# A fused windowed attention and SwiGLU kernel on one Trainium2 core: the first keys by the hardware DMA queues in fp32, and a new order of the second group's turns

## The chip, the cores and the metric

The kernel runs on one core of a Trainium2 chip. The metric is the device time of one execution in microseconds (us). Timed runs come in rounds with the kernel before, and each ratio has a 95% interval. Profile times are us from the start of the profiled execution's span. The span is about 1.7 us shorter than the time of the run.

## The reference

```python
# q, k, v: (4, 8, 768, 64) float32; n_sink = 4, window = 128
scores = scale * q @ k^T
keep   = (key position < n_sink) or (0 <= query position - key position < window)
a      = softmax(where(keep, scores, -1e9))
x      = (a @ v), heads side by side: 3072 tokens x 512
g      = x @ w_gate; val = x @ w_val          # 512 -> 1536
out    = (silu(g) * val) @ w_out              # 1536 -> 512, float32
```

## The kernel before

Tokens are handled in 12 groups of 256. Keys and queries arrive with tokens on the partitions and are "turned" by TensorE: a small matmul with an identity matrix transposes each block, then ScalarE (keys) or VectorE (queries) copies it from PSUM to SBUF as bf16. One "pair" is two heads. Group 0 opens the kernel, so its turns cannot begin before its first keys and queries have landed. The parts that matter here:

```python
# loads of group 0
nat[0] = natp.tile([P, H, 4 * D], BF16, tag="kq", name="kq")
for k2 in range(2):                       # keys: two cast loads, fp32 to bf16
    hs = slice(4 * k2, 4 * k2 + 4)
    nc.gpsimd.dma_start(nat[0][0:64, hs], four_tokens(k, 0, hs))
first = []
for p in range(NP2):                      # queries: four plain loads, fp32
    st = opool.tile([P, 2, 4 * D], FP32, tag="ot", name="st")
    (nc.scalar, nc.sync)[p % 2].dma_start(
        st[64:P], four_tokens(q, 0, slice(2 * p, 2 * p + 2)))
    first.append(st)
# ... index patterns on GpSimd, then the values, group 1's keys and queries, weights (all cast)

# the opening, in program order (each engine keeps this order)
warm(8)                                   # matmuls of zeros
build_masks()                             # also the two identities
first_T(0)                                # turn of pair 0: keys and queries
first_T(1)
step_S(0, 0)                              # scores and exponentials, pair 0
step_S(0, 1)
first_T(2); first_T(3)                    # cut: masks between
step_S(0, 2); step_S(0, 3)
# ... probabilities times values, first half
for ph in range(2):
    step_T(1, ph, (0,))                   # group 1's keys, both halves
step_X(0, 0)                              # transpose of group 0's output
step_T(1, 0, (1,), nc.scalar.copy)        # group 1's queries, first half
step_X(0, 1)
step_T(1, 1, (1,), q_late=True)           # queries, second half
step_S(1, 0, 1)                           # scores and exponentials of group 1
```

In `step_T` the keys' copy goes to ScalarE at once. With `q_late` the queries' copy goes to VectorE after the work already put off there.

The softmax here doesn't subtract the row's maximum and nothing guards it: scores larger than these inputs give would overflow.

## Time and profile before

| what | value |
|---|---|
| time, median of 3 | 240.22 us (240.15 to 240.7) |
| profiled run | 239.81 us, span 238.1 us |
| TensorE busy | 231.4 us, 97% of the span |
| first turn starts | 4.95 us |
| first exponential starts | 6.62 us |
| group 1's first exponential starts | 14.68 us |
| dense matmuls start, on the chain | 22.97 us |

The prediction below shows the chain of waits. Two lines of the timeline of before complete it. Columns are start, length, engine, line, operation, output and input, count, and in brackets the idle time before and what ended it.

```profile
5.74 0.84 ACT L264 CAST kT<-pt 128x256 bf16<-128x256 f32 x2 [2.02 <-PE pt L258]
...
6.62 1.64 ACT L337 ACTIVATE e<-s 128x384 bf16<-128x384 f32 x4
```

ScalarE copies the keys of pairs 0 and 1 in one stretch (two copies, 0.84 us) and then begins the exponentials at once.

### The profile page before, as it was taken

How to read it: one execution, taken by the hardware profiler on the slowest of the kernel's cores; microseconds unless marked ns; L12 is line 12 of the kernel's file. 1: busy time of each engine (PE TensorE's matmuls, PEld its weight loads, DVE VectorE, ACT ScalarE, POOL GpSimd, SP SyncE). 2: the span in 40 equal slices, each digit the busy share in tenths (PEclk: the TensorE clock that was granted, in tenths of full speed). 3: DMA queues.
4: the chain of work that ended last, by engine and by line, in shares of the span. 5: the costliest groups of instructions: out<-in, count | busy, mean ns of one | idle time of the engine just before them, and what ended most of it. 6: DMA issues, size and time to landing. Idle time of an engine off the chain costs nothing.

```text
span 238.1 us, 5212 instructions
## 1 busy us (share of the span) xinstructions
PE 231.4 (97%) x2071; PEld 135.2 (57%) x2083; DVE 158.7 (67%) x337; ACT 113.3 (48%) x230; POOL 70.4 (30%) x90
## 2 busy tenths in 40 slices
PE   7899999999999999999999999999999999999994
PEld 3578887678655455544445554445454455488444
DVE  4779788749953798960798961598961599877000
ACT  2988339257732665412755622656622663333222
POOL 8976397406908049300808000000000000000000
PEclk9999999999999999999999999999999999999999
DMA  7999999997999999959999926600204200200132
GB/s 140 171 186 195 204 190 204 166 220 67 145 168 188 185 167 135 134 56 239 119 150 78 160 53 173 117 0 4 44 9 126 88 0 3 44 0 3 48 130 88
DMA packets 98936, 27.37 MB, mean 115 GB/s; under 512 B 84832, under 2 KB 95968, under 8 KB 98912
## 3 DMA queue, kind: packets, MB, share of 16 engines
q0 software_dynamic: 68832, 13.90, 70.7%
q1 hardware_dynamic: 29504, 12.69, 25.2%
q10 hardware_dynamic: 576, 0.46, 0.6%
q8 instruction: 16, 0.26, 0.4%
q14 instruction: 8, 0.07, 0.1%
HBM read 28.34 MB, written 6.29 MB: 145 GB/s over the span
## 4 chain that ended last, share of the span: by engine, by line
PE 91%; ACT 4%; DMA 2%; DVE 1%; issue 1%; DVEq 0%; POOLq 0%
PE pv L450 26%; PE pg L450 25%; PE pd L504 25%; PE o L386 5%; PE s L331 5%; ACT e L337 3%; PE pt L258 2%; DMA kq<-in_k_dram 2%; PE pd L485 1%; PE px L422 1%; DVE e L342 1%; ACT xn L394 1%; PE pk L360 1%; ACT th L457 0%; DVE qT L264 0%
## 5 line engine op out<-in xcount | busy, mean ns | idle before, releaser
L450 PE MATMUL pv<-xT,wv 128*128 128x256 bf16 (+1 forms) x384 | 74.4, 326 | 0.0
L450 PE MATMUL pg<-xT,wg 128*128 128x256 bf16 (+1 forms) x384 | 74.2, 326 | 0.0
L457 ACT ACTIVATE th<-pg 128x512 f32<-128x512 f32 x72 | 43.7, 607 | 59.7 <-PE pg L450 59.2
L464 DVE SCALAR_TENSOR_TENSOR u<-th,pg 128x512 bf16<-128x512 f32 x72 | 49.2, 683 | 30.7 <-ACT th L457 30.0
L504 PE MATMUL pd<-wo,ht 128*128 128x512 bf16 x265 | 62.4, 379 | 0.5
L465 DVE TENSOR_TENSOR ht<-u,pv 128x512 bf16<-128x512 bf16 x72 | 49.5, 688 | 9.6 <-PE pv L450 3.2
L450 PEld LDWEIGHTS <-wg 128*128 128x128 bf16 x384 | 37.4, 98 | 25.4 <-issue 0.2
L337 ACT ACTIVATE e<-s 128x512 bf16<-128x512 f32 (+1 forms) x96 | 46.2, 578 | 0.9 <-PE s L331 0.8
L450 PEld LDWEIGHTS <-wv 128*128 128x128 bf16 x384 | 34.1, 98 | 20.3 <-issue 3.6
L504 PEld LDWEIGHTS <-ht 128*128 128x128 bf16 x276 | 25.8, 98 | 28.0 <-issue 0.2
L508 ACT ACTIVATE ot<-pd 128x512 f32<-128x512 f32 x23 | 13.7, 597 | 53.2 <-PE pd L504 50.8
L342 DVE TENSOR_TENSOR e<-e,mask 128x1024 bf16<-128x1024 bf16 (+2 forms) x49 | 29.1, 631 | 2.1 <-ACT e L337 2.0
L106 POOL DMA_DIRECT2D kq<-in_k_dram x16 | 14.4, 901 | 49.2 <-DMA kqT<-kq 48.2
L122 POOL DMA_DIRECT2D va<-in_v_dram x24 | 21.6, 919 | 2.0 <-DMA kq<-in_q_dram 0.6
L398 DVE TENSOR_TENSOR xn<-o,rcp 128x256 bf16<-128x256 f32 x44 | 18.7, 425 | 4.2 <-DMA xT<-xn 2.7
L386 PEld LDWEIGHTS <-e 128*128 128x128 bf16 x352 | 16.6, 98 | 6.7 <-DVE e L342 0.9
L386 PE MATMUL o<-va,e 128*128 128x65 bf16 x352 | 18.2, 193 | 0.5 <-DVE e L342 0.4
L106 POOL DMA_DIRECT2D kq<-in_q_dram x16 | 14.5, 906 | 1.0 <-DMA wo<-in_moe_w_out_dram 1.0
L391 DVE RECIPROCAL rcp<-o 128x4 f32<-128x4 f32 x48 | 8.3, 176 | 5.3 <-PE o L386 5.1
L489 DVE TENSOR_SCALAR ot<-pd 128x128 f32<-128x128 f32 x1 | 0.3, 292 | 14.4 <-PE pd L485 14.4
L331 PE MATMUL s<-kqT 64*128 64x128 bf16 (+1 forms) x168 | 9.3, 238 | 0.0
L386 PE MATMUL o<-vsb,es 128*128 128x260 bf16 x32 | 8.8, 274 | 0.1
(59 smaller groups left out, 104.1 us busy)
## 6 DMA issues: line engine op xcount, KB each, us to landing
out_dram<-ot SPq DMA_DIRECT2D x23, 256.0 KB
va<-in_v_dram POOLq DMA_DIRECT2D x24, 128.0 KB, 6.4
kq<-in_k_dram POOLq DMA_DIRECT2D x18, 128.0 KB, 4.4
kq<-in_q_dram POOLq DMA_DIRECT2D x16, 128.0 KB, 5.2
wo<-in_moe_w_out_dram POOLq DMA_DIRECT2D x4, 384.0 KB, 12.4
wg<-in_moe_w_gate_dram POOLq DMA_DIRECT2D x4, 256.0 KB, 8.2
wv<-in_moe_w_val_dram POOLq DMA_DIRECT2D x4, 256.0 KB, 8.8
kq<-in_k_dram POOLq DMA_DIRECT2D x3, 256.0 KB, 8.9
```

What stands on the lines that cost most here:

```text
L106: nc.gpsimd.dma_start(x[:, j, i].rearrange("p (h d) -> p h d", d=D), src[b, :, t0:t0 + P].rearrange("h m d -> m h d"))
L122: nc.gpsimd.dma_start(va[:, j, :, 0:D], v[b, :, t0:t0 + P].rearrange("h m d -> m h d"))
L331: nc.tensor.matmul(pss[2 * i + h][:, col:col + n * P], keys(b, t, r, p), queries(g, r, p, j, n), start=True, stop=True)
L337: nc.scalar.activation(e_t[g][:, 2 * p + h, lo:512], pss[2 * i + h][:, lo:512], AF.Exp, scale=scale)
L342: nc.vector.tensor_tensor(e, e, m[:, :, lo:512].broadcast_to([P, e.shape[1], 512 - lo]), op=ALU.mult)
L386: nc.tensor.matmul(o, l, r, start=(i == 0), stop=(i == len(mms) - 1), skip_group_check=True)
L398: nc.vector.tensor_tensor(xns[g, j][:, 256 * hh:256 * (hh + 1)].rearrange("p (h d) -> p h d", h=4), po[:, :, 0:D], rcp.broadcast_to([P, 4, ...
L450: nc.tensor.matmul(ps[:, i * n:(i + 1) * n], ws[fi][:, c, fo * P:(fo + 1) * P], x[:, 0:n // P, c], start=(c == 0), stop=(c == DMC - 1))
L457: nc.scalar.activation(th, pg, AF.Tanh, scale=0.5)
L464: nc.vector.scalar_tensor_tensor(u, th, 1.0, pg, op0=ALU.add, op1=ALU.mult)
L465: nc.vector.tensor_tensor(hts[tb][:, f:f + two].rearrange("p a n -> p (a n)"), u, pv, op=ALU.mult)
L504: nc.tensor.matmul(po, hts[tb][:, f, ts * P:(ts + 1) * P], wos[f // n][:, f % n], start=(f == 0), stop=(f == DFC - 1))
```

## The change

The intent: keys 0 and 1 come over ScalarE's and SyncE's hardware queues instead of waiting for the software queue's cast load. Later, the second half of group 1's keys is turned together with its queries, since keys and queries use different halves of the array; this puts the first output transpose ahead of it.

```diff
-    for k2 in range(2):
-        hs = slice(4 * k2, 4 * k2 + 4)
-        nc.gpsimd.dma_start(nat[0][0:64, hs], four_tokens(k, 0, hs))
-    first = []
-    for p in range(NP2):
-        st = opool.tile([P, 2, 4 * D], FP32, tag="ot", name="st")
-        (nc.scalar, nc.sync)[p % 2].dma_start(
-            st[64:P], four_tokens(q, 0, slice(2 * p, 2 * p + 2)))
-        first.append(st)
+    nc.gpsimd.dma_start(nat[0][0:64, 4:8], four_tokens(k, 0, slice(4, 8)))
+    first = [opool.tile([P, 2, 4 * D], FP32, tag="ot", name="st") for _ in range(NP2)]
+    for n, (p, src) in enumerate(((0, q), (0, k), (1, k), (1, q), (2, q), (3, q))):
+        o = slice(0, 64) if src is k else slice(64, P)
+        (nc.scalar, nc.sync)[n % 2].dma_start(
+            first[p][o], four_tokens(src, 0, slice(2 * p, 2 * p + 2)))
     ... first_T(p): for p < 2 the keys come from first[p], with the fp32 identity
-    for ph in range(2):
-        step_T(1, ph, (0,))
+    step_T(1, 0, (0,))
     step_X(0, 0)
     step_T(1, 0, (1,), nc.scalar.copy)
     step_X(0, 1)
-    step_T(1, 1, (1,), q_late=True)
+    step_T(1, 1, q_late=True)
```

More of the change, by code (lines that the diff above doesn't have):

```diff
@@ L583, in first_T @@
     def first_T(p):
+        cast = p > 1
         evict = turn(0, (p,), (0, 1),
-                     lambda i, p: first[p] if i else nat[0][:, 2 * p:2 * p + 2],
-                     (ident, id32))
+                     lambda i, p: nat[0][:, 2 * p:2 * p + 2] if cast and i == 0 else first[p],
+                     (ident if cast else id32, id32))
         evict(0, nc.scalar.copy)
```

## The prediction

> **What bounds the kernel now.** I read first the page's busy times, to see whether one engine fills the span; then the chain of work that ended last, over the first 45 us, because the change touches only the opening; then the DMA queues in half-microsecond windows around 4 us. From the page:
>
> ```profile
> PE 231.4 (97%) x2071; PEld 135.2 (57%) x2083; DVE 158.7 (67%) x337; ACT 113.3 (48%) x230; POOL 70.4 (30%) x90
> ```
>
> TensorE is full. From the stretches of the trace, it is busy 36.95 us of the 37.00 between 23 and 60 us and 59.8 of 60 in each of the next two. So whatever the opening gains or loses moves all that follows by as much and reaches the end in full; nothing later has slack to swallow it. The opening itself is a chain over several engines:
>
> ```profile
> 1.31 3.59 DMA kq<-in_k_dram
> ...
> 4.95 0.81 PE pt L258 x21
> ...
> 5.78 0.44 DVE qT L264
> ...
> 6.26 0.37 PE s L331 x4
> 6.63 1.63 ACT e L337 x4
> 8.26 0.27 ACT kT L264
> ...
> 11.07 0.45 PE o L386 x9
> 11.52 1.01 PE pt L258 x32
> 12.53 0.33 PE px L422 x4
> 12.86 0.56 PE pt L258 x16
> 13.42 0.33 PE px L422 x4
> 13.75 0.56 PE pt L258 x16
> 14.32 0.37 PE s L331 x6
> 14.69 2.05 ACT e L337 x4
> ...
> 20.93 1.76 ACT xn L394 x8
> ...
> 22.97 0.87 PE pv L450 x8
> ```
>
> Columns are start, length and work. The cast load of group 0's first keys lands at 4.90 us; until then TensorE has no real work. After 6.63 us ScalarE's exponentials carry the chain; from 11.52 to 14.32 TensorE does (transposes of group 1's keys and queries, L258, and of group 0's output, L422); then ScalarE, VectorE and ScalarE again until 22.7 us, from where TensorE is dense. Two spots can therefore move the time: when the first exponential starts (6.63), and when group 1's first exponential starts (14.69).
>
> **What the skill says, and whether the trace agrees.** The Trainium skill, "DMA: Bandwidth & Descriptors", section "SWDGE vs HWDGE vs iDMA", gives casting during a DMA to GpSimd's software path alone. That is why the moved keys arrive in fp32. Its section "Queues, rings and completion order" says that each DMA engine goes round-robin over the queues it has work for and drains a whole packet before it switches. The trace agrees in pattern. At 3.5 to 4.0 us the software queue alone works, and at 4.0 to 4.5 us ScalarE's hardware queue (q10) gets its turn, though its second load had been issued by 2.2 us:
>
> ```profile
> q0 software_dynamic: 160, 0.08, 121.0%
> q1 hardware_dynamic: 7, 0.00, 2.6%
> ...
> q10 hardware_dynamic: 107, 0.10, 61.9%
> q0 software_dynamic: 81, 0.03, 53.1%
> q1 hardware_dynamic: 17, 0.02, 10.5%
> ```
>
> (Packets, MB, share; the first two lines are the earlier window.) The third place is "TensorE: Matmul & The Clock Gate", section "The mechanism" of part 3: matmuls on different row groups of the array overlap. The trace agrees: in group 2's turn 32 transposes, keys in one half and queries in the other, take 0.57 us (33.47 us on the chain), as long as the 16 of one kind alone at 12.86 us (0.56 us).
>
> **Part by part.**
>
> A. The loads. Before, two software cast loads bring four key pairs' halves and each hardware queue brings two fp32 query pairs. From the records of the loads' completion counts, the first key load lands at 4.90 us and the second at 6.94; the queries of ScalarE's queue land at 3.66 and 5.89, those of SyncE's at 4.29 and 6.23. Note the second loads: each lands about 2 us behind the first of its queue. After, ScalarE's queue carries queries 0, keys 1, queries 2; SyncE's carries keys 0, queries 1, queries 3; one software load brings keys 4 to 7 in the same place and at the same time (1.31 us) as the first did.
>
> A1, the first turn. It needs queries 0 (3.66), keys 0 (SyncE's first, 4.29) and the fp32 identity. The identity ends at 4.02 us now (3.37 + 0.65); it comes earlier by the 0.7 us of GpSimd's removed issue. So the first turn starts at about 4.3 instead of 4.95: 0.65 us sooner. Its 8 pairs are spaced about 0.058 us (from the starts at 5.19 to 5.77), set by the fp32 query half; an fp32 key half beside it on other rows should not lengthen that.
>
> A2, the second turn. Today it follows the first at once, since its queries come by SyncE's first load (4.29) and its keys by the load that the first turn waits for too (4.90). After the change keys 1 and queries 1 are the second loads of their queues, and I expect them where the second loads land today, 5.89 and 6.23 us. TensorE and ScalarE are in order: the second turn stands before the first scores, and both key copies on ScalarE stand before the first exponential. From the start of a turn to its copy takes 0.79 us (4.95 to 5.74), a copy 0.42 (0.84 for two). So the first exponential starts at 6.25 + 0.79 + 0.42 + 0.04 = 7.50 instead of 6.62: a loss of 0.88 us. The gain of A1 lies wholly beside this.
>
> A3, turns three and four. Queries 2 and 3 become third loads; one more round puts them near 7 to 8 us. They are needed only when the four exponentials end (7.50 + 1.64 = 9.14 us). Hidden, I think.
>
> B. Group 1's keys. Before, TensorE runs keys(both halves) 1.01, output 0.33, queries 0.56, output 0.33, queries 0.56 between 11.52 and 14.32. After, the second half's keys ride with its queries, 32 transposes in 0.57, so one stretch of about 0.5 us goes: the scores start near 13.8. But ScalarE now copies those late keys (0.56 us, 1.12 for two) just before the exponential. The turn ends near 13.85, the copy runs 13.9 to 14.47, and the exponential starts at about 14.48 instead of 14.68. B is worth 0.2 us, not 0.5; the rest becomes waiting of TensorE before 22.7 us, where ScalarE sets the pace.
>
> Sum: +0.88 - 0.20 = +0.68 us; 240.22 + 0.68 = 240.9. I take 240.8, shading toward rival 1.
>
> **Rivals.**
> 1. The second hardware loads come sooner. With keys 1 and queries 1 landed by about 5.0, the exponentials would start at 6.25 or so and the change would gain 0.4 + 0.2 = 0.6 us: 239.6. For it: removing one software load takes a competitor away, and the round-robin is inferred. Against: the surviving software load is the same size at the same time, and the second loads wait behind exactly that one.
> 2. Later still. Behind the second hardware loads now come values in 128-byte pieces rather than keys in 512-byte ones, up to 64 pieces an engine; the records show about 1075 such packets a us, so nearly 1 us for a load. If the completion of queries 1 or the third loads wait behind it, another 0.3 us goes: 241.2.
> 3. fp32 keys and fp32 queries don't overlap. Each turn would take about 0.93 instead of 0.46 us (16 x 0.058): 0.4 us more on the second turn, 241.3. The bf16 pairs' overlap speaks against it.
> 4. The transfers are hidden anyway. If ScalarE had slack before its exponentials, A would be worth nothing and B 0.2: 240.0. The chain's unbroken line from 4.95 to 6.63 us speaks against it.
>
> **Range and chances.** The terms are all under 1 us of 240, and runs of the kernel before spread from 240.15 to 240.7. Rival 1 (239.6) sets the low end; rivals 2 and 3 (241.2, 241.3) with 0.3 us of spread between runs the high one: 239.7 to 241.6. A change of 2% is 4.8 us, about as much as the whole opening waits; I give 0.005 to faster and 0.01 to slower, the rest to within 2%. Within that, slower than before has about 0.7.
>
> **What would show it.** In the profile after: the first turn starts near 4.3 us; TensorE then waits about 1.3 us on a hardware load of keys or queries between first and second turn; the first exponential starts near 7.5 us; group 1's first exponential follows ScalarE's copy of the late keys with almost no gap, near 15.2 us; the dense gate and value products start near 23.6 instead of 22.97. If the second turn starts before 5.5 us, step A2 is wrong and the time falls. If group 1's exponential starts over 0.4 us sooner after the output products than before, B is under-sized. If the span moves by more than the shift of those products, something after 23 us was touched that I held fixed, most likely the order in which weights and keys land.

## The result, and the profile after

In the first measurement the changed kernel took 240.55 us (median of 4, 240.43 to 240.76) beside 240.36 us of the kernel before. The ratio is 1.0008, interval 0.999 to 1.0025. In a second one with five rounds it took 240.95 us beside 240.29, ratio 1.0029 (1.0017 to 1.0041). A ratio is the mean time of one kernel's fast runs over the mean of the other's fast runs of the same rounds, so it is not quite the ratio of the medians quoted. Both measurements lie within 2% and within the stated range. The second is clear of 1 and puts the loss near 0.7 us.

On the page TensorE is busy 232.3 us of a span of 239.1 us, again 97%. The timeline of after shows the opening:

```profile
4.50 0.69 PE L256 MATMUL pt<-id,st 64*64 64x64 f32 x32
...
6.29 1.10 PE L256 MATMUL pt<-id,st 64*64 64x64 f32 x32 [1.09 <-DMA st<-in_k_dram]
...
7.42 0.37 ACT L262 CAST kT<-pt 128x256 bf16<-128x256 f32 x1 [1.80 <-PE pt L256]
...
7.69 1.65 ACT L335 ACTIVATE e<-s 128x384 bf16<-128x384 f32 x4
```

The first turn starts 0.45 us sooner than before. The second then waits 1.09 us for keys 1. Its copy ends the wait of ScalarE, and the first exponential starts at 7.69 instead of 6.62 us, 1.07 us later. The chain of waits of after tells the second spot (start, length, what):

```profile
4.98 8.56 DMA kq<-in_q_dram
...
13.59 0.64 PE pt L256 x16
14.22 0.33 PE px L420 x4
14.55 0.73 PE pt L256 x32
15.28 0.57 ACT kT L262
15.85 1.97 ACT e L335 x4
...
22.01 1.75 ACT xn L392 x8
...
24.04 0.87 PE pv L448 x8
```

The late keys are indeed turned together with the queries (x32). ScalarE's copy of them then stands before the exponential, as forecast. A new line leads the chain: the load of group 1's queries, issued at 4.98 us and landed at 13.54. Before, it was issued at 5.61 and landed at 12.08. The group of the key and query tiles gives the same in short. First before, then after; the longest of the landing times is this load's:

```profile
DMA to landing us min/median/max: 3.6/5.1/6.5
```

```profile
DMA to landing us min/median/max: 3.8/6.9/8.6
```

From the start of the dense products to the end nothing changed beyond 0.1 us: 238.1 - 22.97 = 215.1 us before, 239.1 - 24.04 = 215.1 us after.

One thing to keep in mind for all that follows. The two profiles differ by 1.0 us of span, while the timed means differ by 0.2 and 0.7 us. The profiled run of before (239.81 us) lay under its kernel's median, and that of after (240.76) over its own. A profile is one execution. I use profiles to see which wait ends where, and the rounds for what it is worth.

### The profile page after: what moved, and what is told of

Read it like the earlier page. It is cut to its first block, busy times and chain, and to the rows that moved or that the text cites. A ratio compares the mean times of both kernels' runs of the same rounds, so it can differ in the third digit from the quotient of the medians.

```text
span 239.1 us, 5257 instructions
## 1 busy us (share of the span) xinstructions
PE 232.3 (97%) x2099; PEld 134.7 (56%) x2099; DVE 159.0 (66%) x337; ACT 113.2 (47%) x230; POOL 69.6 (29%) x89
## 3 DMA queue, kind: packets, MB, share of 16 engines
HBM read 28.34 MB, written 6.29 MB: 145 GB/s over the span
## 4 chain that ended last, share of the span: by engine, by line
PE 90%; DMA 4%; ACT 3%; POOL 1%; DVE 1%; issue 0%; POOLq 0%; DVEq 0%
PE pv L448 26%; PE pg L448 25%; PE pd L502 25%; PE o L384 5%; PE s L329 4%; DMA kq<-in_q_dram 4%; ACT e L335 2%; PE pt L256 1%; PE pd L483 1%; POOL va L122 1%; ACT xn L392 1%; PE px L420 1%; PE pk L358 1%; POOL kq L164 0%; DVE e L340 0%
## 5 line engine op out<-in xcount | busy, mean ns | idle before, releaser
L502 PE MATMUL pd<-wo,ht 128*128 128x512 bf16 x276 | 63.5, 379 | 0.0
L262 DVE CAST qT<-pt 128x512 bf16<-128x512 f32 (+1 forms) x9 | 5.0, 571 | 6.8 <-PE pt L256 6.8
```

What stands on the lines that cost most here:

```text
L502: nc.tensor.matmul(po, hts[tb][:, f, ts * P:(ts + 1) * P], wos[f // n][:, f % n], start=(f == 0), stop=(f == DFC - 1))
```

## The experiments

Theory 1: keys 1 and queries 1, being second in their queues, hold the second turn and with it the exponentials; the new order of turns is worth at most 0.2 us. Its reason for the lateness was that the second loads wait, round-robin, behind the software queue's packets. Rivals: the profiles' difference is spread between executions; the second load of a queue is late by itself; or all queues share one rate, so cutting the loads differently is no help.

Twelve kernels ran, all with correct results. The last three columns are read from each run's profile, the query load's landing from its completion counts. The kernels ran in three sets, each on another chip, so a row is to be compared with the kernel before beside it.

| run | median us (before beside it) | ratio, 95% interval | first exp. | group 1's first exp. | group 1's queries land |
|---|---|---|---|---|---|
| same_before | 240.34 (240.29) | 0.9999 (0.9987 to 1.0012) | 6.68 | 14.74 | 11.62 |
| loads_only | 240.89 (240.29) | 1.0032 (1.0009 to 1.0054) | 7.75 | 15.91 | 13.13 |
| turns_only | 240.21 (240.29) | 1.0003 (0.998 to 1.0026) | 6.61 | 14.40 | 12.11 |
| same_after | 240.95 (240.29) | 1.0029 (1.0017 to 1.0041) | 7.88 | 16.19 | 13.42 |
| late_cast | 241.47 (240.42) | 1.0026 (0.9993 to 1.0059) | 8.65 | 16.78 | 13.51 |
| one_load | 241.69 (240.42) | 1.0049 (1.0013 to 1.0084) | 7.82 | 15.93 | 13.82 |
| turns_dve | 240.07 (240.42) | 0.9981 (0.995 to 1.0013) | 6.57 | 14.48 | 11.84 |
| late_cast_dve | 241.25 (240.42) | 1.0044 (1.0007 to 1.0082) | 8.18 | 16.10 | 13.62 |
| quiet | 240.29, one run (240.62) | none | 7.44 | 15.24 | 12.71 |
| after_warm | 240.96 (240.62) | 1.0011 (0.9986 to 1.0036) | 7.87 | 16.24 | 13.50 |
| mirror | 240.66 (240.62) | 0.9992 (0.9964 to 1.002) | 6.90 | 15.46 | 13.52 |
| turns_dve2 | 240.23 (240.62) | 0.9982 (0.9957 to 1.0008) | 6.73 | 14.35 | 12.12 |

### same_before and same_after: is it spread?

No edit.

> The kernel before, once more, to measure the spread. Theory 1 (the second hardware loads hold the second turn): the first exponential starts again near 6.6 us and group 1's near 14.7 us, and the time is within 0.2 us of the kernel before. Rival (spread: the first profile of before happened to catch early landings; it ran in 239.81 us where the median is 240.36): the first software key load lands later than 4.90 us here, the first exponential starts 0.5 us or more later than 6.62, and the profiled span is nearer 238.7 than 238.1 us.

> The changed kernel once more. Theory 1: the second turn again waits about 1.1 us for keys 1 and the first exponential starts between 7.5 and 7.9 us; the time is 0.2 to 1.0 us over the kernel before. Rival (spread): the second hardware loads land more than 0.5 us apart from the first profile's 6.24 and 6.65 us, and the time differs from the kernel before by less than 0.1 us.

The kernel before repeats its opening to within 0.06 us (6.68 and 14.74 us), and its ratio to itself is 0.9999. The changed kernel again starts its first exponential late (7.88 us) and is slower by 0.29%. The late opening is therefore the kernel's, not the execution's.

The profile of same_after holds a further loss. The table of stretches, with the granted clock in the column PEclk (the others are the stretch, its length and the busy times with counts), reads:

```profile
5.20:8.60 3.40, 2.19 (x81) 1.55 (x75) 0.85 (x2) 1.36 (x4) 3.33 (x7) 1.00 2.03 178
8.60:12.00 3.40, 3.29 (x64) 2.31 (x57) 2.24 (x5) 2.85 (x9) 2.91 (x4) 0.50 1.67 193
```

From 8.6 to 12.0 us the clock stood at half. The second four exponentials then start 2.85 us after the first instead of 2.34 as in the first profile of after: 0.5 us more. The first profile of after has no such stretch, although TensorE was busy for less of the one before it (1.94 of 3.40 us against 2.19). So a late opening went with a second loss in one of these two executions; that the wait is the reason is not shown.

### loads_only and turns_only: one part each

loads_only is the changed kernel with the old order of group 1's turns; turns_only is the kernel before with the new order:

```diff
# loads_only, against the changed kernel   (turns_only makes the reverse edit to the kernel before)
-    step_T(1, 0, (0,))
+    for ph in range(2):
+        step_T(1, ph, (0,))
     step_X(0, 0)
     step_T(1, 0, (1,), nc.scalar.copy)
     step_X(0, 1)
-    step_T(1, 1, q_late=True)
+    step_T(1, 1, (1,), q_late=True)
```

> Part A alone: keys 0 and 1 by the hardware queues, the old order of group 1's turns. Theory 1: the first exponential starts near 7.7 us as in the changed kernel, and the time is about 0.2 to 1.0 us over the kernel before and equal to or up to 0.2 us over the changed one. Rival (the two parts cancel: the loads are neutral and the new order of turns costs something): the same time as before within 0.1 us.

> Part B alone: the loads of before, group 1's late keys with the late queries. Theory 1 as I forecast it: group 1's first exponential starts 0.2 us sooner after the output products (14.5 against 14.68 us) and the time falls by 0.2 us. Rival (the copy of the late keys on ScalarE takes back all that TensorE gains): 14.7 us and no change of time, within 0.1 us.

The loads alone carry the loss: 1.0032, that is 0.77 us. The chain of loads_only starts

```profile
1.61 5.10 DMA st<-in_q_dram
6.75 0.75 PE pt L256 x30
7.50 0.35 ACT kT L262
7.86 1.54 ACT e L335 x4
```

so here queries 1 (landed at 6.71 us) are the last to come, where in the first profile of after TensorE was seen waiting for keys 1 (6.24) first. Both are second loads of a hardware queue.

The turns alone behave in the trace almost to the digit as forecast. The chain of turns_only:

```profile
13.30 0.63 PE pt L258 x32
13.93 0.57 ACT kT L264
14.50 1.97 ACT e L337 x4
```

The prediction said copy from 13.9 to 14.47 and exponential at 14.48. In time the part is not seen: 1.0003 with a wide interval, which one run of 241.85 us among six has stretched; the medians differ by 0.08 us.

Put side by side, the two parts do not add. From the first output transpose to group 1's first exponential, turns_only takes 14.40 - 12.01 = 2.39 us. The changed kernel takes 15.74 - 13.10 = 2.64. In the changed kernel the query transposes now come just when the query load lands (13.54), so 0.1 to 0.15 us goes into that wait; the 32 transposes take 0.73 us on the chain rather than 0.63. That is the difference of 0.25 us. The fairest measure of part B beside the loads is loads_only, which differs from the changed kernel by part B alone: from the first exponential to group 1's it takes 15.91 - 7.75 = 8.16 us there and 15.74 - 7.69 = 8.05 in the changed kernel. So part B is worth 0.11 us in company, and 0.27 alone (8.06 before, 14.40 - 6.61 = 7.79 in turns_only). These are single profiles, and the same distance differs by 0.29 us between turns_dve and turns_dve2, which are one kernel.

### late_cast, one_load and quiet: why the second loads are late

```diff
# late_cast: the cast load behind the two index patterns
-    nc.gpsimd.dma_start(nat[0][0:64, 4:8], four_tokens(k, 0, slice(4, 8)))
     ...
     nc.gpsimd.iota(tk, [[0, 1]], base=0, channel_multiplier=1, ...)
+    nc.gpsimd.dma_start(nat[0][0:64, 4:8], four_tokens(k, 0, slice(4, 8)))
# quiet: as late_cast, and six more patterns before the cast load (1.6 us later than after)
+    for _ in range(6):
+        nc.gpsimd.iota(idle, [[1, P]], base=0, channel_multiplier=0, ...)
# one_load: pairs 0 and 1 in one load per queue (cut: pairs 2 and 3, and the views of pairs 0 and 1)
+    nc.scalar.dma_start(both[64:P], four_tokens(q, 0, slice(0, 4)))
+    nc.sync.dma_start(both[0:64], four_tokens(k, 0, slice(0, 4)))
```

> The changed kernel with the remaining cast load issued after the two index patterns instead of before them, some 0.5 us later (near 1.85 us instead of 1.31). Theory 1 with the round-robin: the second hardware loads waited behind the cast load's packets, so now they slip ahead of it: keys 1 land near 4.8 us and queries 1 near 5.3 instead of 6.2 and 6.7, the first exponential starts near 6.3 to 6.6 us, and the time falls by about 1.0 us against the changed kernel, to 0.2 or 0.3 us below the kernel before. Rival (the second load of a hardware queue comes late by itself, because its descriptors are made late): the second loads still land after 5.9 us, the first exponential stays near 7.7 us, and the time stays about 0.6 us over the kernel before.

> The changed kernel with pairs 0 and 1 in a single load per queue (256 KB each: queries by ScalarE's queue, keys by SyncE's), so that the second turn needs no second load. If being second in its queue is what makes keys 1 and queries 1 late (theory 1, and its rival too), both turns find their data near 4.6 to 5.2 us, run one behind the other, and the first exponential starts at 6.3 to 6.9 us; the time is within 0.2 us of the kernel before. If instead the late landings are bandwidth (all queues share one rate), the single loads land near 6 us and the time stays 0.6 us over.

> The changed kernel with GpSimd kept busy by six more index patterns before its first load, so that the cast load and everything behind it is issued about 1.5 us later still (near 3.4 us); only the landings of the hardware loads are of interest. If the second load of a hardware queue waits for the software queue's packets (theory 1, round-robin), its packets now follow the first loads at once, from about 3.4 us, and keys 1 land before 5.0 us. If a hardware queue's second load starts late by itself, its packets start again near 4.0 us; with no software writes beside it, keys 1 still land sooner than 6.2 us, near 5.0 to 5.5 us, if it is those writes that hold back the completion.

My expectation for late_cast failed, and so did its edit in part. The index patterns now ran from 0.90 us, so the cast load was issued at 1.44 us instead of 1.31, a delay of 0.13 us and not of 0.5. Even so ScalarE's second load started earlier, at 3.47 us instead of 4.00, and the cast load landed at 7.36 us instead of 5.14. But the second loads did not land earlier: keys 1 at 6.76 and queries 1 at 7.01 us. The first exponential was the latest of all (8.65 us), and that is not the loads' doing alone: in this execution an fp32 transpose took 311 ns up to 10 us, where those of after take 218 from the first turn on. The profiled execution (241.97 us) was also the slowest of six that spread from 240.26 us, so its opening does not stand for the others. Quiet, which issued the cast load at 3.0 us, is the stronger test of the reason. These are the DMA queues between 3.4 and 4.0 us (packets, MB, share), after first, then quiet:

```profile
q0 software_dynamic: 183, 0.09, 120.5%
q10 hardware_dynamic: 1, 0.00, 4.2%
q1 hardware_dynamic: 11, 0.01, 4.1%
```

```profile
q10 hardware_dynamic: 79, 0.07, 59.2%
q1 hardware_dynamic: 35, 0.03, 28.6%
```

With the software queue silent, ScalarE's second load does start at once: its first packet comes at 3.21 us instead of 4.00. So in the changed kernel its start does wait for the cast load's packets. But the landing barely moves, and neither outcome for keys 1 (before 5.0, or 5.0 to 5.5 us) came true: keys 1 at 6.15 us against 6.24, queries 1 at 6.40 against 6.65. In the three other profiles with the loads of after (same_after, loads_only, after_warm) they land at 5.67 to 6.29 and 6.71 to 6.84 us, so keys 1 gained nothing beyond the spread and queries 1 a few tenths. In quiet ten of the sixteen completion counts of keys 1 are in by 4.96 us and the last comes at 6.15. In that time the third loads, queries 2 and 3, are moving on the same queues. The six hardware loads of 128 KB each ran from 2.30 to 6.44 us, which works out at 786 KB in 4.14 us, 190 GB/s. For most of that time the software queue had nothing in flight.

one_load says the same from another side, by the second of its outcomes. With no second load in the way, queries 0 and 1 landed at 4.73 us but keys 0 and 1 only at 6.07. The first turn waited as well, and the first exponential came at 7.82 us. However the first four hardware pieces are cut and whatever runs beside them, the last of them lands at 6.07 to 7.01 us. The second half of theory 1 (they wait for the software queue) is thus not what sets the landing. The third alternative, one rate that all queues share, fits better. Between 2.2 and 6.6 us all queues together move 206 to 226 GB/s in every kernel, however the loads are cut (211 in before, 206 in one_load). The stretch's line, after first and then quiet, has GB/s in its last column:

```profile
2.20:6.60 4.40, 3.31 (x41) 1.39 (x39) 2.23 (x8) 1.86 (x3) 4.40 (x8) 1.00 1.14 217
```

```profile
2.20:6.60 4.40, 4.12 (x49) 2.00 (x51) 1.47 (x7) 1.86 (x3) 4.26 (x8) 1.00 1.02 211
```

Against such a rate the change has a cost that the prediction did not count. A cast load of 128 KB, counted as written, brings the keys of two pairs in bf16; in fp32 the same 128 KB bring one pair. Keys and queries of pairs 0 and 1 are 384 KB before and 512 KB after, and after, the cast load's 128 KB for pairs 2 and 3 move among them. No run varied the bytes alone, so this reading is argued and not shown, and what sets the rate I have not found out.

### mirror: the other choice of keys

```diff
# against turns_dve (below): one cast load for pairs 0 and 1, hardware queues for keys of pairs 2 and 3
-    for k2 in range(2): ... two cast loads
+    nc.gpsimd.dma_start(nat[0][0:64, 0:4], four_tokens(k, 0, slice(0, 4)))
+    for n, (p, src) in enumerate(((0, q), (1, q), (2, q), (3, q), (2, k), (3, k))): ...
```

> The other choice of keys: one cast load brings keys 0 to 3 (pairs 0 and 1) first, the hardware queues bring all queries and, as third loads, keys of pairs 2 and 3 in fp32; turns and copies as in the version with the late keys' copy on VectorE. If what counts is which bytes stand in the early places, the first exponential starts at 6.6 us as in the kernel before, the third loads (near 7.2 to 7.8 us) are hidden behind the exponentials, and the time equals that version's, 0.2 to 0.4 us below the kernel before. If using the hardware queues for keys is bad in itself (slower packets, later loads of group 1), it is 0.5 us or more over that version.

The first turn starts at 4.95 us as in the kernel before, and the first exponential at 6.90. That is 0.28 us later, because the first transposes ran slower: one takes 0.31 us up to 5.5 us and 0.24 from 5.7 us. So the order of the bytes was what mattered for the first exponential. But mirror's median lies above that of turns_dve2, 240.66 against 240.23 us; their intervals against the kernel before overlap, so in time the difference is not shown; it lies between the two outcomes. In the profiles it is 1.1 us at group 1's first exponential (15.46 against 14.35). In mirror TensorE waits for group 1's queries, as its list of waits shows (total us, times, longest):

```profile
PE pt L255 <- DMA kq<-in_q_dram: 0.9, 1, 0.9
```

They landed at 13.52 us, although the software queue had one load fewer ahead of them. All eight runs with keys on the hardware queues and the cast load issued before 2 us have them at 13.1 to 13.8 us (after itself 13.54); all five with cast keys alone at 11.6 to 12.1; quiet has them at 12.71, although it issues that load 1.2 us later than after does. So in these arrangements keys on the hardware queues go with a query load that lands more than 1 us later. It is not the moved keys alone: counted from its issue the load takes 6.47 us in before, 8.56 in after and 6.56 in quiet, which moves the same keys. The moved keys add 128 KB, at 210 GB/s about 0.6 us by estimate, which explains a part at most. The rest is open: the records give queues but not engines, and I found no experiment among these that separates the candidates.

### turns_dve, turns_dve2 and late_cast_dve: the late keys' copy on VectorE

```diff
# in step_T
         if 0 in which:
-            evict(0, nc.scalar.copy)
+            if q_late:
+                later.append(A(evict, 0, nc.vector.tensor_copy))
+            else:
+                evict(0, nc.scalar.copy)
```

> The kernel before with part B alone, and the late keys' copy moved from ScalarE to VectorE. If that copy takes back what TensorE gains (it ran from 13.93 to 14.50 us just before the exponential), group 1's first exponential now starts near 14.2 us instead of 14.50 with part B alone and 14.7 before; the time falls by 0.4 us against before. Rival (VectorE's later start of sink keys and masks becomes the wait): the exponential starts sooner but the dense products still start near 22.8 us, and the time stays within 0.1 us of part B alone.

> The kernel before with part B and the late keys' copy on VectorE, once more, for a narrower interval: 0.2 to 0.4 us below the kernel before (ratio 0.9985), with group 1's first exponential near 14.4 us. Rival: the earlier result was spread, and the ratio is 1.000.

> Both: the changed kernel with the cast load after the index patterns and the late keys' copy on VectorE. If both theories hold, the first exponential starts near 6.3 us and group 1's near 13.9 us; the time is 0.6 to 0.8 us below the kernel before (ratio 0.997). If the cast load doesn't matter, 0.4 us over it.

The chain of turns_dve no longer holds the copy:

```profile
13.26 0.57 PE pt L258 x32
13.83 0.27 PE s L334 x3
14.16 0.30 PE s L334 x3
14.48 2.06 ACT e L340 x4
```

ScalarE now waits for the scores, until 14.48 us, rather than for its own copy, which ends on the chain of turns_only at 14.50. I had expected 14.2. Nothing is gained at this spot, and the dense products start at 22.78 us, against 22.77 in turns_only. So in this profile the copy did not take back the gain; it lay beside the scores. The profile of turns_dve2 shows the rival instead. Its exponential starts at 14.35 us, but the chain leads over VectorE, through the late copies and the sink keys (ks), and the dense products start at 22.80 us:

```profile
13.42 0.63 PE pt L258 x32
14.04 0.68 DVE kT L264
14.72 0.60 DVE qT L264
15.32 0.07 DVE ks L315
```

The time is 0.9981 and 0.9982 of the kernel before in two sets of rounds, both intervals just reaching 1.000 or a little over. It is the fastest version here by its medians against the kernel before beside it, but no single set proves it faster than the kernel before. Against the changed kernel it was not timed in the same rounds.

late_cast_dve put together one idea that failed (the cast load behind the patterns) and one that is neutral, and it is slower: 1.0044. Its profile, too, has transposes of 311 ns up to 10 us.

### after_warm: is the granted clock worth saving?

```diff
     first_T(0)
+    warm(4)
     first_T(1)
```

> The changed kernel with four matmuls of zeros between the first and the second turn, in the 1.1 us in which TensorE waits. If the idle stretch costs a second time by losing the granted clock in some executions (0.5 from 8.59 to 12.0 us in one profile of the changed kernel), this removes that: the first exponential stays at 7.6 to 7.9 us, the second four exponentials start 2.3 us behind it, and the time is 0.1 to 0.4 us below the changed kernel's (near 240.5 us, ratio 1.001). If the clock doesn't matter, the same 240.8 us.

Inconclusive. The ratio is 1.0011 with an interval that holds both 1.000 and the changed kernel's 1.0029. Its chain does show by the way what holds the first turn:

```profile
1.26 3.60 PE wm L241 x8
4.86 0.85 PE pt L256 x32
```

The eight opening matmuls of zeros end at 4.86 us here (4.58 in the first profile of after) and the first turn follows them, though its keys had landed at 4.37.

## Why the prediction was right

The prediction gave 240.8 us in 239.7 to 241.6; the two measurements gave 240.55 and 240.95.

- **The bound.** Right: from the first dense product to the end both kernels take 215.1 us, so the opening's loss goes through in full.
- **A1, first turn at 4.3 us.** It started at 4.50, and at 4.78 in other runs. Keys 0 landed at 4.21 as forecast from the old landings, but the matmuls of zeros ran until 4.5 to 4.9 us. The step overlooked TensorE's own program order. It cost nothing, since the gain was hidden anyway.
- **A2, the second turn.** The failing of the change is this step, as forecast: TensorE waits 1.09 us (about 1.3 forecast), the first exponential starts at 7.69 us (7.50 forecast), a loss of 1.07 us (0.88 forecast). Queries 1 landed at 6.65 instead of 6.23 us, 0.42 us later; the path from there to the exponential was 0.21 us shorter than forecast (1.04 against 1.25), which leaves the 0.2 us. Rival 2 had named a delay of this kind. The number was right. Of its two supports, "where the second loads land today" held; "wait behind the software load" holds for their start (4.00 against 3.21 us in quiet) and not for their landing (6.24 against 6.15).
- **A3, third loads hidden.** Right: they landed at 7.40 and 7.82 us, and the second set of exponentials follows the first at 2.34 us, against 2.33 before.
- **B, 0.2 us.** Right by itself in the trace (exponential 0.2 to 0.3 us sooner in turns_only; in time not resolved), too large in company: from the first exponential of one group to that of the other the changed kernel takes 8.05 us, 0.11 less than loads_only and only 0.01 less than before (14.68 - 6.62 = 8.06). The step failed in holding the landing of group 1's queries fixed; it moved from 12.08 to 13.54 us. The prediction had named the order of landing as the thing most likely to upset it, but placed it after 23 us.
- **Rivals.** 1 (second loads sooner) fell with every run. 2 (values behind the second loads) was not isolated; quiet, with the values issued at 3.72 instead of 2.42 us, brought queries 1 forward by 0.25 us. 3 (fp32 turns don't overlap) fell: the first turn went from 4.50 us to its copy at 5.25, 0.75 us, against 0.79 before. 4 (hidden anyway) fell by loads_only.
- **The signs.** Of the moments it named, group 1's first exponential came at 15.74 us (near 15.2 forecast, although its own terms add to 7.50 + 8.06 - 0.20 = 15.36), the dense products at 24.04 (23.6 forecast).
- **The sum.** The forecast 0.68 us is close to the 0.7 us of the better measurement, and that closeness is partly luck. In the profiles the loss is 1.07 us at the dense products: A2 was 0.2 us too small and B 0.2 us too large. That the timed means show less (0.2 and 0.7) I can only partly explain: the profiled executions of before were faster than its median, and those of after slower than its own. The rest is open.

## What to carry to other kernels

When loads are moved between queues, ask first which bytes stand in the early places of all queues together: here the cast load had brought both first pairs' keys by 4.9 us, and the change gave that place to keys needed 3 us later. Count the bytes too: the moved keys came in fp32, twice what the cast load wrote for them. In these runs a second load that started up to 0.8 us sooner landed at most a few tenths sooner, or even later; read its landing from the trace before relying on it. And two changes can meet in a third transfer, so time them apart and together.

## What the Trainium skill lacked or had wrong

- "DMA: Bandwidth & Descriptors", section "Queues, rings and completion order": the round-robin by packets fits when a queue's second load starts (3.21 us with the software queue silent, 4.00 us in after). The page gives no rate for many small plain loads issued on both hardware queues together; here six of 128 KB, in rows of 1 KB, took 4.14 us, some 190 GB/s, and all queues together moved 206 to 226 GB/s in every kernel.
- The same page, section "SWDGE vs HWDGE vs iDMA", lets one expect that plain loads are better issued on the hardware queues. Where four heads of keys were needed early, the cast load landed them at 4.85 to 5.01 us in the five runs of the old arrangement. The hardware queues landed the last of the first two pairs' fp32 keys and queries at 6.07 to 7.01 us. The page gives no size for what such loads cost later loads of the software queue; here group 1's queries landed at 13.1 to 13.8 us instead of 11.6 to 12.1.
- "TensorE: Matmul & The Clock Gate", section "HAM oscillation — how this bites in real kernels", states the rule as no idle gaps over about 3.4 us. In same_after the clock was halved for 3.4 us although the longest listed waits of TensorE in the stretch before were 0.50 and 0.42 us; it had been busy 2.19 of 3.40 us. The other profile of the same kernel, with waits up to 1.09 us and 1.94 us busy in the same stretch, kept its clock. So neither the longest gap nor the busy share alone tells the two apart, and what does is open.
